# One PSUM chain for MLP and attention, masks on GpSimd, and column-tiled PV for the last token blocks, in a gated mix of sliding attention and token MLP

## The chip, the cores and the metric

The kernel runs on one core of a Trainium2 chip (trn2). The metric is the device time of one execution in microseconds (us), lower is better. The profile's span is some 1.7 us (at most 2.4) shorter than the device time of the same execution; stages below are read from spans. An execution is marked slow when it is over 1.5% above the fastest of its kernel.

## The reference

```python
# x: 1 x 2048 x 512, bf16; 32 heads of 16; window 256; F = 1376
g = sigmoid((x * gate_w).sum(-1, keepdims=True))
q, k, v = split_heads(x @ wqkv)
scores = where(0 <= i - j < 256, q @ k.T * 16 ** -0.5, -1e9)
a = softmax(scores) @ v  -> merge heads -> @ wo
h = layernorm(x)                          # no scale, no bias
u = gelu(einsum("bsd,sf->bdf", h, w1) + b1)   # mixes along the tokens
y = transpose(einsum("bdf,fs->bds", u, w2) + b2)
return g * a + (1 - g) * y
```

## The kernel before

Every operation is recorded as a task with its engine or engines, its buffers and a priority. A list scheduler (`arrange`, with guessed durations) fixes one order before anything is built; each engine then works through its part of that order strictly in sequence. Tokens are in 16 blocks of 128. For each block there are two half tiles of 16 heads, and each half tile has up to three key blocks. One key block is one *score group*: eight row-tiled score matmuls, two exponentials on ScalarE, a mask on two of three, and 16 PV matmuls. There are 90 score groups, in the same order in every kernel of this study. That gives a ruler: the start of score group 24, of 54 and of 89 (the last) marks how far an execution has come, whatever else moved.

```python
# masks: VectorE or GpSimd, as the scheduler finds
got = [add(f"m{qb}.{hf}.{kb}", {"DVE": 1.2, "POOL": 2.1}, emit_m, ex, ORDER["m"], uses=[e])]
# ... PV: e is the stationary operand, 16 matmuls of 128x17, V with a column of ones
# normalise by the sum (17th column)
rc: nc.vector.reciprocal(out=buf(rd)[:], in_=...)
nm: nc.vector.tensor_tensor(out=buf(ob)[...], in0=buf(o)[...], in1=buf(rd)[...], op=ALU.mult)
to: nc.sync.dma_start_transpose(xo[:, qb, :]..., buf(ob))
# ... the gate: g = gg, (1 - g) / 2 = c1, c2 = (1 - g) * b2
ga: nc.scalar.activation(th[:], buf(gb)[:, 0:NT], ACT.Tanh, scale=0.5)
# ... for each token block: two PSUM chains and two passes over 128x512
b, t = chain(f"y{qb}", mms, dw2 + ugr, ORDER["y"] + qb, "y")            # 11 matmuls
yb: affine(buf(bp), buf(b), c1[:, qb:qb + 1], c2[:, qb:qb + 1])         # bp = c1 * y + c2
mms = [(xo[:, qb, c * P:(c + 1) * P], wo[:, c, :], P) for c in range(4)]
b, t = chain(f"a{qb}", mms, [done["ont", qb], dwo, yb], ORDER["a"], "a")  # 4 matmuls
f:  nc.vector.scalar_tensor_tensor(out=buf(ot)[:], in0=buf(b)[:], scalar=gg[:, qb:qb + 1],
                                   in1=buf(bp)[:], op0=ALU.mult, op1=ALU.add)
# ... loads: x0 | K and Q weights, 1 MB | x1 | V weights, 512 KB | x2 | x3
```

(Names before a colon are the tasks' names.)

The softmax here doesn't subtract the row's maximum and nothing guards it: scores larger than these inputs give would overflow.

## Time and profile before

The median is 234.06 us in the rounds of the change (233.92 to 235.37). VectorE is busy 166.4 us, of which 40.4 are masks and 22.5 the two passes at the end of each token block.

And the rows of VectorE that the change touches:

```profile
L602 DVE TENSOR_TENSOR et<-et,mask 128x2048 bf16<-128x2048 bf16 x33 | 40.4, 1231 | 4.0 <-ACT et L591 3.9
...
L538 DVE TENSOR_SCALAR h<-xo,mv,rstd 128x512 bf16<-128x512 bf16 x16 | 13.7, 901 | 0.0
...
L758 DVE SCALAR_TENSOR_TENSOR ot<-pb,gg,bp 128x512 bf16<-128x512 f32 x16 | 12.0, 751 | 6.9 <-PE pb L468 6.9
L317 DVE TENSOR_SCALAR bp<-pb,c,c 128x512 f32<-128x512 f32 x13 | 10.5, 810 | 18.0 <-PE pb L468 18.0
...
L724 DVE SCALAR_TENSOR_TENSOR ug<-t,uf 128x512 bf16<-128x512 f32 (+1 forms) x11 | 9.4, 850 | 5.9 <-ACT t L719 5.9
```

The reader is to see 33 masks of 1.23 us, and means of 0.90 and 0.85 us in the h and ug rows, which are mixtures of undisturbed operations and of ones stretched past 2 us.

### The profile page before, as it was taken

The numbers are of one execution on the slowest core, as the hardware profiler recorded it, in microseconds if no ns is written. First come the engines' busy times: TensorE is split into PE (matmuls) and PEld (weight loads), VectorE is DVE, ScalarE is ACT, GpSimd is POOL, SyncE is SP. The second block draws the span as 40 slices with busy tenths as digits, with TensorE's granted clock in tenths as the row PEclk, the third lists the DMA queues.
The fourth block names the chain that finished last, engine by engine and source line by source line (L and its number), as shares of the span: only waits on it lengthen the run. The fifth ranks groups of instructions, "written<-read, shape, count | busy, mean of one in ns | idle before, by whom it ended". The sixth has DMA issues, their size and how long they took to land.

```text
span 232.9 us, 6602 instructions
## 1 busy us (share of the span) xinstructions
PE 218.2 (94%) x2856; PEld 107.4 (46%) x2856; DVE 166.4 (71%) x255; ACT 192.7 (83%) x220; POOL 66.9 (29%) x50
## 2 busy tenths in 40 slices
PE   7696999979999999999999958999999999999993
PEld 3232444535465444554445523555555555555551
DVE  3779799999877889578899875555565556666522
ACT  2167496778999998996898997999999999999911
POOL 8326534462200003025005100333333333333300
PEclk9799799999999999999999985999999999999999
DMA  6999999002011082010551071010101010301011
GB/s 223 284 209 287 352 345 253 17 0 49 0 25 25 0 312 74 3 25 3 160 226 23 3 246 28 23 48 25 48 24 48 25 45 25 44 28 48 25 46 45
DMA packets 27757, 21.66 MB, mean 93 GB/s; under 512 B 15728, under 2 KB 25456, under 8 KB 27728
## 3 DMA queue, kind: packets, MB, share of 16 engines
q1 hardware_dynamic: 27568, 21.24, 32.4%
q8 instruction: 22, 0.36, 0.6%
q0 software_dynamic: 160, 0.01, 0.5%
q14 instruction: 7, 0.06, 0.1%
HBM read 15.47 MB, written 2.10 MB: 75 GB/s over the span
## 4 chain that ended last, share of the span: by engine, by line
PE 81%; DVE 9%; ACT 4%; DMA 3%; issue 1%; SPq 0%; DVEq 0%; ACTq 0%
PE pb L468 54%; PE pb L627 15%; PE ps L572 12%; DVE h L538 3%; ACT et L591 3%; DMA wqkv<-in_A_wqkv_dram 3%; DVE stats L522 1%; DVE ug L724 1%; DVE QZ L507 1%; DVE b1c L414 1%; PE pb L672 1%; ACT uf L314 1%; ACT t L719 1%; DVE ot L758 0%; DVE KT L433 0%
## 5 line engine op out<-in xcount | busy, mean ns | idle before, releaser
L591 ACT ACTIVATE et<-ps 128x1024 bf16<-128x1024 f32 x180 | 172.1, 1029 | 9.4 <-PE ps L572 8.3
L606 POOL TENSOR_SCALAR_AFFINE_SELECT et<-et 128x2048 bf16<-128x2048 bf16 x27 | 55.1, 2041 | 135.0 <-ACT et L591 130.0
L468 PEld LDWEIGHTS <-wb 128*128 128x128 bf16 (+2 forms) x352 | 30.7, 99 | 39.4 <-issue 11.6
L627 PEld LDWEIGHTS <-et 128*128 128x128 bf16 x1440 | 42.0, 96 | 14.6 <-issue 7.9
L627 PE MATMUL pb<-VA,et 128*128 128x17 bf16 x1440 | 44.6, 171 | 2.4 <-DVE mv L526 2.2
L468 PE MATMUL pb<-ug,wb 128*128 128x512 bf16 (+1 forms) x176 | 44.2, 389 | 0.0
L468 PE MATMUL pb<-h,wb 128*128 128x512 bf16 (+1 forms) x176 | 43.6, 380 | 0.0
L602 DVE TENSOR_TENSOR et<-et,mask 128x2048 bf16<-128x2048 bf16 x33 | 40.4, 1231 | 4.0 <-ACT et L591 3.9
L572 PE MATMUL ps<-QZ,KT 32*128 32x256 bf16 x720 | 36.2, 276 | 3.7 <-ACT et L591 2.3
L468 PE MATMUL pb<-XT,wqkv 128*128 128x512 bf16 x128 | 33.9, 407 | 2.0 <-DMA wqkv<-in_A_wqkv_dram 2.0
L572 PEld LDWEIGHTS <-KT 32*128 32x128 bf16 x720 | 10.8, 92 | 33.4 <-ACT et L591 17.7
L317 DVE TENSOR_SCALAR bp<-pb,c,c 128x512 f32<-128x512 f32 x13 | 10.5, 810 | 18.0 <-PE pb L468 18.0
L507 DVE TENSOR_TENSOR QZ<-pb,par 128x1024 bf16<-128x1024 f32 x16 | 19.0, 1215 | 3.1 <-PE pb L468 2.9
L468 PEld LDWEIGHTS <-wqkv 128*128 128x128 bf16 x128 | 11.9, 102 | 17.2 <-issue 5.0
L643 DVE RECIPROCAL rd<-pb 128x16 f32<-128x16 f32 x32 | 8.1, 254 | 14.5 <-PE pb L627 14.0
L468 PE MATMUL pb<-wqkv,XT 128*128 128x512 bf16 x64 | 16.0, 380 | 1.4 <-DVE VA L433 1.4
L758 DVE SCALAR_TENSOR_TENSOR ot<-pb,gg,bp 128x512 bf16<-128x512 f32 x16 | 12.0, 751 | 6.9 <-PE pb L468 6.9
L468 PE MATMUL pb<-wo,xo 128*128 128x512 bf16 x64 | 16.4, 377 | 0.0
L432 ACT ACTIVATE KT<-pb 128x512 bf16<-128x512 f32 x10 | 6.0, 601 | 12.3 <-PE pb L468 12.3
L650 DVE TENSOR_TENSOR on<-pb,rd 128x256 bf16<-128x256 f32 x32 | 13.5, 423 | 1.0
L538 DVE TENSOR_SCALAR h<-xo,mv,rstd 128x512 bf16<-128x512 bf16 x16 | 13.7, 901 | 0.0
L724 DVE SCALAR_TENSOR_TENSOR ug<-t,uf 128x512 bf16<-128x512 f32 (+1 forms) x11 | 9.4, 850 | 5.9 <-ACT t L719 5.9
(48 smaller groups left out, 99.6 us busy)
## 6 DMA issues: line engine op xcount, KB each, us to landing
wb<-in_B_w_dram SPq DMA_DIRECT2D x8, 512.0 KB, 8.3
wb<-in_B_w_dram SPq DMA_DIRECT2D x2, 2048.0 KB, 8.0
xo<-in_A_x_dram SPq DMA_DIRECT2D x4, 512.0 KB, 9.6
out_dram<-ot SPq DMA_DIRECT2D x16, 128.0 KB, 1.8
wb<-in_B_w_dram SPq DMA_DIRECT2D x4, 352.0 KB, 8.0
wqkv<-in_A_wqkv_dram SPq DMA_DIRECT2D x1, 1024.0 KB, 6.1
wb<-in_B_w_dram SPq DMA_DIRECT2D x1, 1024.0 KB, 5.4
wqkv<-in_A_wqkv_dram SPq DMA_DIRECT2D x1, 512.0 KB, 9.9
```

The source lines that it names most:

```text
L317: return nc.vector.tensor_scalar(out=out_, in0=in_, scalar1=scale, scalar2=bias, op0=ALU.mult, op1=ALU.add)
L468: nc.tensor.matmul(buf(b)[:rows, :], lhsT=lhsT, rhs=rhs, start=(j == 0), stop=(j == n - 1))
L507: lambda k=k, b=b: nc.vector.tensor_tensor(out=QZ[:, i % NQ, k, :, :], in0=buf(b)[:, None, :].to_broadcast([P, 2, SB]), in1=par[:][:, :, N ...
L538: return nc.vector.tensor_scalar(out=h[:, t_, :], in0=xo[:, t_, :], scalar1=mv[:, t_, 0:1], scalar2=rstd[:, t_:t_ + 1], op0=ALU.subtract, ...
L572: made.append(nc.tensor.matmul(buf(b2[r // 2])[:, (r % 2) * 512 + kk * 256:(r % 2) * 512 + kk * 256 + 256], lhsT=KT[32 * r:32 * r + 32, (k ...
L591: lambda j=j, b2=b2, e=e: nc.scalar.activation(out=buf(e)[:, j * 1024:(j + 1) * 1024], in_=buf(b2[j])[:], func=ACT.Exp, scale=SCALE),
L602: return nc.vector.tensor_tensor(out=view, in0=view, in1=mask[:, int(far), None, :].to_broadcast([P, 16, P]), op=ALU.mult)
L606: return nc.gpsimd.affine_select(out=buf(e), in_=buf(e), pattern=[[0, 16], [-1 if far else 1, P]], compare_op=ALU.is_gt if far else ALU.is ...
L627: made.append(nc.tensor.matmul(buf(o)[:, hl * DV:(hl + 1) * DV], lhsT=buf(e)[:, col:col + 128], rhs=VA[:, kb, head, :], start=(first and h ...
L650: lambda rd=rd, o=o, ob=ob, hf=hf: nc.vector.tensor_tensor(out=buf(ob)[:, hf * 256:(hf + 1) * 256].rearrange("p (h d) -> p h d", d=DH), in ...
L724: lambda u=u, t1=t1, fsz=fsz, fc=fc: nc.vector.scalar_tensor_tensor(out=ug[:fsz, fc, :], in0=buf(t1)[:fsz, :], scalar=1.0, in1=buf(u)[:fsz ...
L758: lambda bp=bp, b=b, ot=ot, qb=qb: nc.vector.scalar_tensor_tensor(out=buf(ot)[:], in0=buf(b)[:], scalar=gg[:, qb:qb + 1], in1=buf(bp)[:], ...
```

## The change

Its intent: one pass over PSUM per token block instead of two; a VectorE that has time; fewer TensorE cycles where the tail is. With z the gate logit, g·a + (1-g)·y = (1-g)·(y + e^z·a). So the attention rows are scaled by 2·e^z when they are normalised, accumulate in the same PSUM bank behind the y matmuls, and one affine pass gives the output.

```diff
-                got = [add(..., {"DVE": 1.2, "POOL": 2.1}, emit_m, ex, ORDER["m"], uses=[e])]
+                got = [add(..., {"DVE": 1.2, "POOL": 2.1} if qb >= ORDER["mq"] else {"POOL": 2.1}, ..., two=True)]   # mq = 16
# ... normalise
-            lambda ...: nc.vector.tensor_tensor(out=..., in0=buf(o)..., in1=buf(rd)..., op=ALU.mult)
+            lambda ...: nc.vector.scalar_tensor_tensor(out=..., in0=buf(o)..., scalar=ez[:, qb:qb + 1],
+                in1=buf(rd)..., op0=ALU.mult, op1=ALU.mult)
# ... token blocks from est = 13 on: V stationary, four heads in four column groups
+    nc.tensor.matmul(buf(o)[32 * r:32 * r + 32, at:at + 128], lhsT=VA[:, kb, head * DV:head * DV + 32],
+        rhs=buf(e)[:, col:col + 128], ..., tile_position=(0, 32 * r), skip_group_check=True)
+    # then on VectorE: transpose 32x32 blocks in PSUM, reciprocal, times e^z, times V rows, transpose into xo
# ... the end
-        b, t = chain(f"y{qb}", mms, ...);  yb: bp = c1 * y + c2
-        b, t = chain(f"a{qb}", ...);       f:  ot = gg * a + bp       # VectorE
+        mms += [(xo[:, qb, c * P:(c + 1) * P], wo[:, c, :], P) for c in range(4)]
+        b, t = chain(f"y{qb}", mms, ..., tail=4, tail_deps=rel[qb] + [dwo], ...)
+        f: affine(buf(ot), buf(b), c1, c2)                            # ScalarE or VectorE
# ... loads
-    dwk = load_w("wqk", 0, 2 * D, 0.01)
+    # four loads of 256 KB: K first half, Q first half, (x1), K second half, Q second half
# ... also: XT's blocks serve as probability buffers 5 to 8 once read; the gate in four parts by exp;
#     squares may go to ScalarE; new PSUM bank lists; a model of the shared port and of tile-mode
#     switches in the scheduler; all priorities found anew
```

## The prediction

> **What bounds the kernel now.** I read the page's busy row first, then busy time cut into stages, then the chain of waits, then the timeline of single engines.
>
> ```profile
> PE 218.2 (94%) x2856; PEld 107.4 (46%) x2856; DVE 166.4 (71%) x255; ACT 192.7 (83%) x220; POOL 66.9 (29%) x50
> PE 81%; DVE 9%; ACT 4%; DMA 3%; issue 1%; SPq 0%; DVEq 0%; ACTq 0%
> ```
>
> The second line is the chain that ended last: mostly TensorE. But matmuls overlap, so 94% is not 94% of the work that could be done. The stages say more (columns: busy us of PE, PEld, DVE, ACT, POOL, granted clock, DMA share, GB/s):
>
> ```profile
> 9.20:52.90 43.70, 39.77 (x388) 17.19 (x390) 38.69 (x64) 29.89 (x37) 19.73 (x14) 0.94 0.81 208
> 52.90:136.30 83.40, 82.41 (x1149) 41.80 (x1148) 69.27 (x101) 76.98 (x92) 14.11 (x8) 1.00 0.23 67
> 136.30:150.80 14.50, 11.85 (x171) 5.72 (x175) 9.00 (x13) 13.08 (x15) 2.00 (x1) 0.76 0.32 108
> 150.80:220.20 69.40, 69.40 (x1048) 35.59 (x1048) 41.63 (x60) 68.88 (x73) 24.05 (x12) 1.00 0.15 36
> 220.20:232.90 12.70, 8.83 (x84) 4.43 (x81) 2.94 (x5) 2.33 (x3) 0.00 (x0) 1.00 0.14 42
> ```
>
> The reader should see five stages: projections, where TensorE and VectorE are both full and ScalarE waits; the first MLP layer (TensorE full, ScalarE nearly); a changeover where TensorE idles and its clock falls to 0.76; the second MLP layer, where ScalarE never stops; and a tail of 12.7 us with ScalarE idle. The fourth stage in one line, then one period of it on TensorE:
>
> ```profile
> 149.22 70.94 ACT L591 ACTIVATE et<-ps 128x1024 bf16<-128x1024 f32 x74
> 206.09 0.40 PE L572 MATMUL ps<-QZ,KT 32*128 32x256 bf16 x8
> 206.42 1.90 PE L468 MATMUL pb<-ug,wb 128*128 128x512 bf16 x8
> 208.25 0.40 PE L572 MATMUL ps<-QZ,KT 32*128 32x256 bf16 x8
> 208.58 0.82 PE L468 MATMUL pb<-ug,wb 128*128 128x512 bf16 x3
> 209.24 0.95 PE L627 MATMUL pb<-VA,et 128*128 128x17 bf16 x32
> 210.13 0.40 PE L572 MATMUL ps<-QZ,KT 32*128 32x256 bf16 x8
> ```
>
> 74 exponentials in 70.94 us: 0.95 to 0.96 us each, back to back. From the starts: eight score matmuls 0.33 us, 32 PV matmuls 0.89 us (0.028 each); full 512-column matmuls take 0.216 elsewhere where they are dense. One half tile (3 score groups, 48 PV, 11 of y, 4 of the output projection) is then 0.99 + 1.33 + 2.38 + 0.86 = 5.56 us of TensorE, against six exponentials at 0.95 = 5.7 us. TensorE and ScalarE are almost equally full. A gain must come from idle time of both, not from one engine's sum.
>
> Where is that idle time? Adding the waits between ScalarE's instructions from 9.2 us (first K copy) to 220.2 us (last exponential) gives 21 us: about 14 before 60 us, 7 later. TensorE's own work, 608 wide matmuls x 0.216 + 1440 x 0.028 + 720 x 0.041 + start-up matmuls and gate (about 6), is 207 us; the other 26 us of the span are waits, slow clock and the two ends.
>
> **What the Trainium skill says.** (1) "SBUF — State Buffer", section "Who interferes with whom": VectorE and GpSimd share a port pair as an exclusive lock; a VectorE operation in a two-port mode, or with two SBUF inputs against a GpSimd operation that reads SBUF, blocks or is blocked for the whole instruction. This trace agrees:
>
> ```profile
> 49.11 2.12 DVE L538 TENSOR_SCALAR h<-xo,mv,rstd 128x512 bf16<-128x512 bf16 x1
> 127.30 2.49 DVE L724 SCALAR_TENSOR_TENSOR ug<-t,uf 128x512 bf16<-128x512 f32 x1
> 127.16 2.09 POOL L606 TENSOR_SCALAR_AFFINE_SELECT et<-et 128x2048 bf16<-128x2048 bf16 x1 [0.88 <-POOL et L606]
> ```
>
> Undisturbed, these two VectorE operations take 0.40 and 0.69 us; each was stretched past 2 us by a POOL mask that started just before (POOL's at 49.08 and 127.16). (2) "TensorEngine Tiling (Array Packing)", sections "Key Properties" and "Restrictions": independent tiles run in parallel, a change of tiling mode drains TensorE, and column tiling disables fast weight load. The row-tiled score groups agree on parallelism (eight in 0.33 us; 256 columns are half of the 0.216 us matmul, so eight in sequence would be 0.86). No column tiling is in this trace. (3) "ScalarE: Activation LUTs", section "What ACT_TABLE_LOAD costs": back-to-back activations overlap by about 93 ns. Here a 1.03 us exponential advances ScalarE by 0.95, a 0.60 copy by 0.50.
>
> **The change part by part.** The instruction orders of both builds were compared engine by engine.
>
> *One PSUM chain.* Attention rows are normalised with exp(gate logit) x 2 and accumulated after the 11 y matmuls in the same bank; one scale-and-bias replaces two passes. Removed: 16 final operations on VectorE (12.0 us), the 16 y evictions (13 on VectorE, 10.5 us; 3 on ScalarE). Added: 16 evictions, 14 on VectorE at 0.81 = 11.3 us. Matmul count unchanged. In the second-layer stage VectorE is only 60% busy, so little there is on the path. In the tail it counts: before, 33 wide matmuls, 48 PV and four evictions follow the last exponential.
>
> *Masks.* 33 VectorE masks (40.4 us) go to GpSimd, which then does 60 x 2.04 = 122 us instead of 55. Two per half tile are 4.1 of 5.7 us, so GpSimd keeps up. The price is the lock: 28 GELU operations with two SBUF inputs still on VectorE. GpSimd holding the port 70% of the time, at about 1 us remaining, is 0.7 us each, about 20 us of waiting, plus the 16 normalisations.
>
> *VectorE's sum.* -40.4 (masks) -12.0 -10.5 +11.3 -3.6 (five squares to ScalarE) +4.5 (six bias evictions from ScalarE) +2.7 (gates) and, for six column-tiled half tiles, -4.0 +12 (two transposes, reciprocal, two products, estimated 2 us from the PSUM rows of 0.42 to 0.75): -40 us. 166 becomes 126, some 150 with the blocking.
>
> *ScalarE's sum.* Before, up to the last exponential: 180 x 0.95 + 17 copies x 0.50 + 11 tanh x 0.52 + 6 bias x 0.58 = 188.7. After: 18 copies, 5 squares, 4 tiny gate exponentials: 189. No gain; only its idle time can shrink.
>
> *TensorE's sum.* 288 of 1440 PV matmuls become column-tiled. Four groups side by side, 128 columns in a quarter of 0.216: 16 take at least 0.22 us; with mode change I take 0.32 instead of 0.44, so 18 groups save 2.2 us: 205 us.
>
> *Order and buffers.* The weight load is split, K's first half ahead (256 KB rather than 1 MB), and XT0's copies go to two engines: the first K matmul waited 1.95 us for weights at 7.59; I take 1 us off. Probability buffers 5 to 9 (XT reused), score banks confined to three pairs. Counting TensorE's work between score groups, six groups a stage (before -> after): 18.1 -> 15.5, 12.8 -> 14.1, 13.3 -> 12.4, 13.7 -> 13.7, 14.6 -> 12.0, 12.4 -> 13.7, 13.3 -> 12.0, 9.6 -> 12.2, then 11.1 -> 11.1 to 12.1, and from group 84 to the end 20.5 -> 17.0. ScalarE needs 11.4 to 13.5 in each. The hump at the projections and the hole at the changeover (measured 14.4 us for 9.6 of work, at half clock) are levelled.
>
> *Tail.* After the last exponential: 48 PV (0.2 wait + 1.0), VectorE's chain about 2.4 beside nine y matmuls (1.9), four projections (1.0), eviction 0.8, store to end 3.0 (229.87 to 232.9 now) and waits: 8.7 against 12.7. Saves 4.0.
>
> *Sum.* ScalarE's view: start 8.0 + work 188.5 + idle + tail 8.7. Idle was 21; levelling takes about 6 to 8 (the hump 2.6, the changeover 3, some of the start), the lock gives back 1 or 2: 15. Total 220. TensorE's view: 205 + start 4 + waits to group 12 of 5 + 4 in the first layer + 2 later + 4.5 at the end = 224.5. The middle is 222 of span; the device time is 1.3 above the span now (234.19 against 232.9), and I lean slightly to the ScalarE view: **222.5 us**, 5% faster.
>
> **The rivals.** (a) *The lock binds.* VectorE was already 38.7 of 43.7 us busy in the projection stage, without many masks of its own; with the port held, bias evictions come late, banks stay taken and score groups wait. For: the 2.12 and 2.49 us rows. Against: the new schedule models the port, VectorE loses 40 us, and nine probability buffers absorb late masks. It would give 227 to 236. (b) *Column tiles do not pay.* Without overlap 16 matmuls take 16 x 0.054 = 0.86 us, 8 us more in the final stages, and the transposes add up to 2 us on the last path. For: no fast weight load. Against: row tiles do overlap here. It would give 228 to 231. (c) *The waits nearly vanish.* ScalarE idle falls to 8 us or less: 213 to 215. For: 52.9 to 136.3 has little idle already. Against: the projections need more TensorE than ScalarE whatever the order. (d) *Fewer VectorE passes are hidden anyway.* In the second-layer stage I believe this; then the gain is only tail and levelling, as in my sum.
>
> **Range and chances.** Rival (c) sets the low end and (a) the high: 214 to 230. Two per cent faster is below 229.5. The tail and levelling are separate gains of 4 and 6 us that both would have to fail: faster 0.88, same 0.10, slower 0.02.
>
> **What would show each step right or wrong.** Tail: last exponential to end about 9 us. Levelling: no changeover stage with clock below 0.9; ScalarE idle about 15 us between first K copy and last exponential; exponentials still near 1.03 us each. Lock: the GELU and h rows' mean above 0.9 us and POOL masks at 2.04 or more. Column tiles: 16 PV in 0.25 to 0.40 us. VectorE busy 140 to 155 us, POOL near 135. If ScalarE idle stays above 20 us with waits on evictions, (a) holds; if PV groups of the last three tiles take over 0.6 us, (b).

## More of the kernel before

The granted TensorE clock in 40 slices (tenths; 9 is nine tenths or more):

```profile
PEclk9799799999999999999999985999999999999999
```

Then stages cut at the score-group marks 24, 54 and 89 (columns: stretch, its length, busy us of PE, PEld, DVE, ACT, POOL, granted clock, DMA share, GB/s):

```profile
0.00:79.63 79.63, 72.49 (x820) 33.82 (x821) 65.67 (x114) 57.21 (x72) 29.93 (x32) 0.96 0.57 151
79.63:150.76 71.13, 67.50 (x908) 33.55 (x909) 56.19 (x77) 64.18 (x75) 12.90 (x6) 0.95 0.29 92
150.76:217.59 66.83, 66.83 (x1031) 34.42 (x1031) 39.66 (x58) 66.35 (x71) 23.18 (x12) 1.00 0.15 36
217.59:232.90 15.31, 11.44 (x102) 5.64 (x101) 4.90 (x7) 4.90 (x6) 0.87 (x1) 1.00 0.15 44
```

I call these the start, the first layer (which ends with the changeover to the second), the second layer, and the end.

## The result, and the profile after

The changed kernel is correct. Its four executions took 223.61, 229.18, 224.80 and 230.22 us, median 226.99; the kernel before 234.06. Ratios in this text are the mean time of one kernel's fast runs over that of the other's in the same rounds, so not quite the ratio of the medians quoted: here 0.9567, interval 0.9494 to 0.964. So the sign and the range were right, but half of the executions were in a slower state at a lower clock (1.0 against 0.981). The profiled execution is the 223.61 us one.

Busy row, chain of waits and clock of the page after:

```profile
PE 212.1 (96%) x2856; PEld 101.9 (46%) x2856; DVE 125.7 (57%) x239; ACT 191.4 (86%) x221; POOL 133.1 (60%) x84
...
PEclk9999999999999999999999999999999999999999
...
PE 86%; DMA 6%; ACT 2%; DVE 2%; SPq 1%; issue 1%; ACTq 0%
```

VectorE lost 40.7 us and the share of VectorE in the chain fell from 9% to 2%. The clock has no dip. The same four stages as before:

```profile
0.00:74.17 74.17, 68.97 (x816) 33.36 (x816) 54.36 (x121) 57.00 (x72) 43.55 (x40) 1.00 0.63 163
74.17:140.94 66.77, 66.07 (x908) 32.65 (x908) 43.47 (x61) 64.05 (x76) 40.80 (x21) 1.00 0.29 96
140.94:211.44 70.50, 70.50 (x1054) 33.01 (x1053) 24.94 (x51) 66.82 (x71) 47.13 (x25) 1.00 0.12 36
211.44:221.90 10.46, 6.58 (x81) 2.92 (x80) 2.92 (x7) 3.49 (x4) 1.64 (x1) 1.00 0.08 27
```

Set against before: start -5.5, first layer -4.4, second layer **+3.7**, end -4.9; together -11.0 us of span. The second layer became longer: matmuls that used to stand in the tail now stand there, where TensorE was already full (busy 66.83 of 66.83 before, 70.50 of 70.50 after). TensorE's timelines account for it, counted from start to start: 197 wide (512-column) matmuls begin in this stage instead of 172 (in the end 24 instead of 45) and take 6.35 us more, the PV matmuls take 2.66 us less, since 15 of their groups are column-tiled, and the score matmuls take the same. That makes the 3.7 us.

The column-tiled PV in the tail, TensorE's timeline (start, length, instruction; modelled ends, so starts are compared):

```profile
213.73 0.59 PE L506 MATMUL pb<-ug,wb 128*128 128x512 bf16 x2
214.26 0.41 PE L783 MATMUL pb<-et,VA 128*32 128x128 bf16 x16
214.49 0.40 PE L783 MATMUL pb<-XT,VA 128*32 128x128 bf16 x16
214.71 0.40 PE L783 MATMUL pb<-et,VA 128*32 128x128 bf16 x16
215.04 2.12 PE L506 MATMUL pb<-ug,wb 128*128 128x512 bf16 x9
```

Sixteen start every 0.225 us, so 48 take 0.78 us with the way back to wide matmuls, where 48 of the old kind took 1.33. What it costs on VectorE follows at once:

```profile
215.16 0.73 DVE L799 STREAM_TRANSPOSE pb<-pb 128x512 f32<-128x512 f32 x1 [2.82 <-PE pb L783]
215.93 0.27 DVE L804 RECIPROCAL pb<-pb 128x16 f32<-128x16 f32 x1
...
216.90 0.45 DVE L831 STREAM_TRANSPOSE xo<-zt 128x256 bf16<-128x256 bf16 x1
```

Two products of 0.18 and 0.42 us are left out. 215.16 to 217.35 is 2.2 us, of which nine y matmuls cover 2.0 (215.04 to 217.00). Finally the rows that the lock could stretch (VectorE), and GpSimd's masks:

```profile
L877 DVE SCALAR_TENSOR_TENSOR ug<-t,uf 128x512 bf16<-128x512 f32 (+1 forms) x11 | 11.7, 1066 | 0.1
...
L577 DVE TENSOR_SCALAR h<-xo,mv,rstd 128x512 bf16<-128x512 bf16 x16 | 5.5, 402 | 0.0
```

```profile
L698 POOL TENSOR_SCALAR_AFFINE_SELECT et<-et 128x2048 bf16<-128x2048 bf16 x40 | 80.9, 2029 | 59.1 <-ACT et L683 47.0 <-PE ps L664 6.0 <-PE pb L720 2.2
L698 POOL TENSOR_SCALAR_AFFINE_SELECT XT<-XT 128x2048 bf16<-128x2048 bf16 x20 | 40.1, 2012 | 17.0 <-ACT XT L683 10.9 <-PE ps L664 3.6 <-PE pb L783 1.7
```

The ug row rose from 0.85 to 1.07 us, the h row fell from 0.90 to 0.40, which is undisturbed: the new order keeps h away from masks and pays at the GELU.

### The profile page after: what moved, and what is told of

Its sections match the earlier page's. It is cut to its first block, busy times and chain, and to the rows that moved or that the text cites.

```text
span 221.9 us, 6636 instructions
## 1 busy us (share of the span) xinstructions
PE 212.1 (96%) x2856; PEld 101.9 (46%) x2856; DVE 125.7 (57%) x239; ACT 191.4 (86%) x221; POOL 133.1 (60%) x84
## 4 chain that ended last, share of the span: by engine, by line
PE 86%; DMA 6%; ACT 2%; DVE 2%; SPq 1%; issue 1%; ACTq 0%
PE pb L506 56%; PE pb L720 14%; PE ps L664 13%; DMA wqkv<-in_A_wqkv_dram 4%; PE pb L783 2%; DMA XT<-in_A_x_dram 2%; ACT et L683 2%; SPq L365 1%; PE pb L594 1%; DVE c L629 1%; DVE KT L470 1%; SPq L360 0%; ACT ot L343 0%; ACT VA L469 0%; DVE c L628 0%
## 5 line engine op out<-in xcount | busy, mean ns | idle before, releaser
L683 ACT ACTIVATE et<-ps 128x1024 bf16<-128x1024 f32 x120 | 116.1, 1028 | 8.0 <-PE ps L664 6.6
L698 POOL TENSOR_SCALAR_AFFINE_SELECT et<-et 128x2048 bf16<-128x2048 bf16 x40 | 80.9, 2029 | 59.1 <-ACT et L683 47.0
L683 ACT ACTIVATE XT<-ps 128x1024 bf16<-128x1024 f32 x60 | 58.3, 1027 | 4.6 <-PE ps L664 4.2
L698 POOL TENSOR_SCALAR_AFFINE_SELECT XT<-XT 128x2048 bf16<-128x2048 bf16 x20 | 40.1, 2012 | 17.0 <-ACT XT L683 10.9
L346 DVE TENSOR_SCALAR ot<-pb,c,c 128x512 bf16<-128x512 f32 x14 | 11.3, 810 | 27.9 <-PE pb L506 27.9
L720 PEld LDWEIGHTS <-et 128*128 128x128 bf16 x800 | 23.3, 96 | 7.0 <-issue 3.3
L720 PE MATMUL pb<-VA,et 128*128 128x17 bf16 x800 | 25.5, 171 | 1.0 <-DVE KT L470 1.0
L345 DVE TENSOR_SCALAR uf<-pb,b1c 128x512 f32<-128x512 f32 (+1 forms) x11 | 8.2, 749 | 11.9 <-PE pb L506 11.8
L744 DVE SCALAR_TENSOR_TENSOR on<-pb,ez,rd 128x256 bf16<-128x256 f32 x26 | 12.6, 484 | 0.9 <-DMA xo<-on 0.2
L561 DVE BATCH_NORM_STATS2 stats<-xo 128x6 f32<-128x512 bf16 x16 | 10.6, 681 | 2.6 <-DMA xo<-in_A_x_dram 2.6
```

What stands on the lines that cost most here:

```text
L345: return nc.vector.tensor_scalar(out=out_, in0=in_, scalar1=bias, scalar2=None, op0=ALU.add)
L346: return nc.vector.tensor_scalar(out=out_, in0=in_, scalar1=scale, scalar2=bias, op0=ALU.mult, op1=ALU.add)
L561: f"bs{t_}", {"DVE": 0.67}, lambda b=b, t_=t_: nc.vector.bn_stats(buf(b)[:], xo[:, t_, :]),
L683: lambda j=j, b2=b2, e=e: nc.scalar.activation(out=buf(e)[:, j * 1024:(j + 1) * 1024], in_=buf(b2[j])[:], func=ACT.Exp, scale=SCALE),
L698: return nc.gpsimd.affine_select(out=buf(e), in_=buf(e), pattern=[[0, 16], [-1 if far else 1, P]], compare_op=ALU.is_gt if far else ALU.is ...
L720: made.append(nc.tensor.matmul(buf(o)[:, hl * DV:(hl + 1) * DV], lhsT=buf(e)[:, col:col + 128], rhs=V4[:, kb, head, :], start=(n_ == 0 and ...
```

## The experiments

Three questions were open. Is the gain the change's work, or the clock dips that it happens to remove? Which part makes which stage's gain? And where does the slower half of the executions come from? My theory at first: levelling (an order without humps) and the tail. The rivals: the clock alone, and the lock or VectorE.

Twelve runs were made, all correct, each in five rounds with 6 to 22 executions; one is the changed kernel unaltered. First the table of what they gave; group marks are from the one profiled execution, whatever its state. That is allowed for the three later stages only, because they turned out the same in both states (rows "after" and "unaltered").

| run | median, us | ratio of fast runs | start | first layer | second layer | end |
|---|---|---|---|---|---|---|
| before | 234.06 | 1 | 79.6 | 71.13 | 66.83 | 15.31 |
| after | 226.99 | 0.957 | 74.2 | 66.77 | 70.50 | 10.46 |
| before_warm | 231.29 | 0.988 | 77.7 | 69.76 | 66.83 | 15.38 |
| after_warm | 228.18 | 0.974 | 79.5 | 66.76 | 70.50 | 10.46 |
| after_nocol | 232.26 | 0.992 | 81.9 | 66.77 | 69.47 | 13.32 |
| after_twice | 232.10 | 0.989 | 81.0 | 66.76 | 72.05 | 11.15 |
| after_again (unaltered) | 229.71 | 0.964 | 79.9 | 66.76 | 70.50 | 10.40 |
| after_oneload | 227.82 | 0.963 | 78.5 | 66.77 | 70.50 | 10.14 |
| after_vearly | 229.72 | 0.972 | 83.1 | 66.77 | 70.50 | 10.48 |
| before_split | 239.75 | 1.008 | 85.3 | 71.97 | 66.83 | 15.07 |
| after_fix | 226.69 | 0.970 | 76.8 | 66.77 | 70.50 | 10.47 |
| after_onelate | 224.58 | 0.961 | 77.0 | 66.77 | 70.50 | 10.15 |
| after_mhalf | 232.19 | 0.983 | 78.2 | 69.43 | 70.50 | 10.40 |
| after_onelast | 232.90 | 0.994 | 84.9 | 66.77 | 70.50 | 10.11 |

### before_warm: the old kernel without its clock dips

The kernel before with 33 dummy matmuls of zeros (weight loads 2889 instead of 2856; where 28 is said of them, that is a miscount) put into six of TensorE's waits; every other instruction keeps its order.

```diff
+    fills = {"k0_0.0": 9, "pv0.0.0": 9, "s9.0.9": 4, "s9.0.7": 6, "pv8.1.8": 1, "s9.0.8": 4}
+        for n_, t in enumerate(plan):
+            if fills.get(t.name):
+                fill(n_, fills[t.name])      # matmuls of zeros into a PSUM bank that is free there
```

> The kernel before with 28 dummy 512-column matmuls at six places where TensorE waits (9 ahead of the first K chain, 9 ahead of the first PV group, 15 around the changeover to the second layer), every other instruction in the same order. Clock theory: a good part of the 10.4 us gained comes from the granted clock (0.971 before, 1.0 after); then this alone is 3 to 6 us faster than the kernel before (228 to 231 us) with a clock of 0.985 or more. Levelling theory: the dips fall where other engines set the time; 0 to 1 us faster (233 to 234.5), even at a higher clock.

231.29 us, ratio 0.988 (0.9836 to 0.9925). Its first two stages (the granted clock is the number after POOL's):

```profile
0.00:77.73 77.73, 72.55 (x826) 35.21 (x839) 65.61 (x114) 57.21 (x72) 29.98 (x32) 1.00 0.59 155
77.73:147.49 69.76, 68.33 (x913) 34.29 (x923) 56.17 (x77) 64.18 (x75) 12.91 (x6) 1.00 0.31 94
```

So the dips, and with them what follows from them, cost the old kernel 2.8 us (1.2% of 234), between the two expectations; in the two profiles' stages it is 1.9 in the start and 1.4 at the changeover. "TensorE: Matmul & The Clock Gate" in the Trainium skill, "Part 1: The HAM clock gate", says that a window of idleness of some 3.4 us halves the clock, and that the windows run freely so that the point of the switch varies from run to run. At the changeover of the kernel before, the clock was 0.50 from 137.63 to 144.46 us. In the 3.41 us ahead of that, TensorE was busy for 1.62 us, so about 1.8 us of idleness were enough in this case, less than the page's window. But the sum of the idleness does not decide either: in the control below (after_again) 1.0 us idle in the 3.37 us from 29.60 was followed by half clock, while in after_mhalf 1.6 us idle in the 3.40 us from 136.20 was not. What does decide stays open here. That the clock varies between executions agrees (0.964 to 0.985 in the runs of the kernel before beside this one). This is a measure for what follows: at full clock, from mark 24 to the end, the old kernel needs 151.97 us and the new one 147.73. That is -4.2: first layer -3.0, second layer +3.7, end -4.9.

### after_warm: dummies in the changed kernel's largest early wait

```diff
+    fills = {"v0.0": 8}
```

> The changed kernel with 8 dummy matmuls in the 1.8 us in which TensorE waits for V's weights, nothing else. If the runs of 229 to 230 us at clock 0.981 come from a clock dip after this early wait, all runs are at 223.5 to 225 us with clock 1.0. If the dip starts elsewhere, some runs stay at 229 to 230.

228.18 us, clocks 0.989 to 1.0, start 79.5. The second expectation is the nearer one: no execution is at 225 us or below, and the slowest took 228.97. The dummies did not hold the clock in the profiled execution: TensorE still waited 2.35 us behind them, for V weights that let it go on at 15.93 us, and from 16.47 to 19.89 us the clock was half. But the start is late without that too: one execution had clock 1.0 and still took 226.79 us, against 223.61 and 224.80 for the good executions at the same clock. A slow start is thus a late start first; the clock comes second.

### after_nocol: no column tiles

```diff
-    ... est=13.0 ...
+    ... est=16.0 ...
```

The scheduler places everything anew from there.

> The changed kernel with plain PV for the last three tiles too (rescheduled; the POOL order is the same). My theory: column tiling saves 6 x 0.55 us of TensorE, of which half is on the path, and the tail loses VectorE's short chain for a DMA transpose of over 2 us: 2.5 to 4.5 us slower than the changed kernel (226 to 228 in its fast state), tail over 9.5 us. Rival, that it is worth nothing: within 1 us.

Second layer and end of this run:

```profile
148.71:218.18 69.47, 68.49 (x1029) 35.00 (x1041) 17.86 (x36) 67.20 (x72) 45.93 (x24) 1.00 0.14 38
218.18:231.50 13.32, 9.65 (x93) 4.86 (x93) 1.56 (x4) 3.98 (x5) 2.73 (x2) 0.96 0.14 40
```

Without tiles the end is 2.9 us longer and the second layer 1.0 shorter: the tiles are worth 1.9 us net, under my 2.5 to 4.5 and over the rival's 1. How much of it is TensorE's time and how much the DMA transpose that the tiles avoid is not told apart. The total of 232.26 says more (5 us) only because this run's start is 2 us later than that of the slow unaltered profile; TensorE's weight loads come in the same order for the first 2359 of 2856, up to 184 us in the changed kernel, so the edit is not in the start.

### after_twice: each output bank evicted twice

```diff
+                affine(bp[:], buf(b), c1[:, qb:qb + 1], c2[:, qb:qb + 1]),     # a dummy fp32 pass
                 affine(buf(ot), buf(b), c1[:, qb:qb + 1], c2[:, qb:qb + 1]),
```

> The changed kernel, in which each output bank is evicted twice (a dummy pass of 0.8 us ahead of the real one), nothing else moved: the second VectorE pass that the merged PSUM chain took away, put back. My theory: VectorE has room in the second layer, only the last eviction is on the path: 0.8 to 1.5 us slower. Rival, that the removed pass is the gain: 3 us or more slower.

```profile
147.80:219.85 72.05, 69.16 (x1043) 33.16 (x1056) 34.21 (x63) 67.03 (x71) 47.09 (x25) 1.00 0.12 33
219.85:231.00 11.15, 6.42 (x80) 2.91 (x80) 3.44 (x10) 4.83 (x6) 1.62 (x1) 0.94 0.11 36
```

+1.55 us in the second layer and +0.75 at the end, 2.3 together, although VectorE is busy only 34 of 72 us there. My number was 0.8 to 1.5, the rival's 3 or more; neither holds, and mine missed the larger part. A bank is held longer, and TensorE waited 1.4 us for evictions that it had not waited for. So a second pass is not all hidden here. (In the kernel before, the two passes stood on two banks; here both hold one bank, so this is not the old form put back exactly.)

### after_again: the unaltered changed kernel, as control

> The changed kernel unaltered, as the control of this set. In the earlier sets V's weights landed 8.7 us after issue in the run of 223.6 us, but 11.9 to 12.2 us in three variants, whose TensorE then waited to 16 us and ran at half clock. If that is a state of the changed kernel itself, here too the runs split: 223.5 to 225 with clock 1.0, and 228 to 231 with clock 0.975 to 0.993. If it belongs to the variants, all are at 223.5 to 225.

Six executions from 224.79 to 231.96: the split belongs to the changed kernel itself, as the first expectation has it, though one execution (227.20) lies between the two states. Its profile is of the slow state:

```profile
0.00:79.94 79.94, 72.79 (x818) 34.44 (x819) 54.56 (x121) 57.29 (x72) 43.52 (x40) 0.96 0.64 151
79.94:146.70 66.76, 66.06 (x909) 32.67 (x909) 43.49 (x61) 64.04 (x76) 40.79 (x21) 1.00 0.30 96
146.70:217.20 70.50, 70.50 (x1055) 33.03 (x1055) 24.94 (x52) 66.81 (x71) 47.13 (x25) 1.00 0.12 36
217.20:227.60 10.40, 6.58 (x81) 2.92 (x80) 2.91 (x7) 3.49 (x4) 1.63 (x1) 1.00 0.08 27
```

Compare with the four lines of the good execution: from mark 24 on they agree within 0.07 us. The whole difference between the two states, 5.8 us, is in the start. And its first sign is a load. The issues of the weights in the good execution, then in this one (KB each, us from issue to landing):

```profile
wqkv<-in_A_wqkv_dram SPq DMA_DIRECT2D x4, 256.0 KB, 5.2
...
wqkv<-in_A_wqkv_dram SPq DMA_DIRECT2D x1, 512.0 KB, 8.7
```

```profile
wqkv<-in_A_wqkv_dram SPq DMA_DIRECT2D x4, 256.0 KB, 7.7
...
wqkv<-in_A_wqkv_dram SPq DMA_DIRECT2D x1, 512.0 KB, 12.0
```

The V weights land 3.3 us later, and score group 0 begins at 17.07 instead of 13.72, 3.35 later. The other 2.4 us come later in the start, where this execution has a half-clock stretch (0.62 at 32 to 36 us; another, 0.63 at 8 to 12, lies ahead of group 0). This is one profile of each state. And the late V weights are not all of it: in after_mhalf, whose loads are the same, they landed 7.4 us after issue and group 0 began at 12.42, earlier than in the good execution, and yet the start took 78.2 us. In the rest of the experiments I therefore attack the start.

### after_oneload, after_vearly, before_split: three ways to load the weights

The first issues K and Q weights in one load of 1 MB, as the kernel before did; the second keeps the split but issues all five weight loads ahead of x1; the third gives the split to the kernel before and nothing else.

```diff
# after_oneload
+        if t.name == "wk0":
+            t.emit = lambda: nc.sync.dma_start(wqkv[:, :, 0:2 * D], ...)
+        elif t.name in ("wq0", "wk1", "wq1"):
+            t.emit = lambda: None
# after_vearly: wk1, wq1 and wv moved ahead of x1 in the fixed order
# before_split
+        if t.name == "wqk":
+            t.emit = lambda: part((512, 768), (0, 256))
+        elif t.name == "wv":
+            t.emit = lambda: part((768, 1024), (256, 512), (1024, 1536))
```

> The changed kernel with Q's and K's weights in one load of 1 MB as in the kernel before, all else in the same order. Theory that the split loads (rows of 512 B) delay V's weights in some runs: V's weights land at 12 to 12.5 us in every run, first scores at 14 to 14.5, all runs 224 to 226. Theory that the delay comes from elsewhere in the changed kernel: runs still reach 228 to 231.

> The changed kernel with all five weight loads ahead of the second block of x, all else in the same order. Theory that V's weights wait behind other loads: they land by 10 to 11 us, TensorE does not wait at 11 us, first scores at 12.5 to 13, clock 1.0, all runs 222 to 224, so 1 us below the best of the changed kernel and 5 to 7 below its slow runs. Rival, that the projections are bound by VectorE and the XT transposes: no better than 224.

> The kernel before with the changed kernel's split of the weight loads and nothing else. Theory that this split is a risk and no gain: V's weights land later than 12.3 us in most runs, 234 to 238 us. Rival, that it is part of the gain (the first K matmul at 6.5 us rather than 7.6): 232.5 to 233.5.

One load put the V weights at 7.9 us from issue and group 0 at 12.51, but the median was 227.82 and the executions still reached 230.25, as the second expectation has it. A new wait stood in VectorE's queue (timeline of VectorE, wait in brackets), and behind it one of TensorE:

```profile
18.64 1.32 DVE L452 CAST b2c<-b2t 128x16 f32<-128x16 bf16 x1 [3.02 <-DMA b2t<-in_B_b_dram]
```

```profile
21.42 0.40 PE L664 MATMUL ps<-QZ,KT 32*128 32x256 bf16 x8 [2.79 <-DVE KT L470]
```

A cast of a bias vector that nothing needs before the second layer blocks a K copy that the next score group needs. With the weights early it was worse (229.72, the rival's side), for the same reason with another load:

```profile
14.74 0.69 DVE L561 BATCH_NORM_STATS2 stats<-xo 128x6 f32<-128x512 bf16 x1 [6.46 <-DMA xo<-in_A_x_dram]
```

```profile
16.61 1.89 PE L506 MATMUL pb<-wqkv,XT 128*128 128x512 bf16 x4 [5.25 <-DVE QZ L546]
```

The statistics of token block 4 wait 6.5 us for the x block that was moved back, and the Q copies of block 0 stand behind them. The split alone did not help the old kernel: its two fast executions are 0.8% slower (1.0023 to 1.013), and four of six were slow, with a median of 239.75 us. In the profile, a slow one, the first K chain does start earlier, at 6.95 us instead of 7.59, but then TensorE waits 4.7 us for the V weights. So in the old order the split is no gain: what it wins at the first K chain it loses behind the V weights. "DMA: Bandwidth & Descriptors" of the Trainium skill, "Measured", gives 6.15 us for a load of 1 MB and asks for loads of that size. Its figure is for loads issued from GpSimd and counts the time that the DMA engines are busy; here SyncE issues, and the time is from issue to landing. With this difference the case comes close: 5.8 to 6.1 us for the K and Q weights in one load. Of four quarters, each took a median of 4.8 to 7.7 us. The V weights behind four quarters took 6.9 to 12.2 us over the runs, those behind one load 7.9 to 9.9: behind the split some landed late and some did not, and what makes them late is not shown. (The sets of rounds ran on different chips of the machine, which is not ruled out.)

### after_fix and after_onelate: the same loads with VectorE's early queue put in another order

Both move eight VectorE tasks that wait for x1 or for the biases behind block 0's Q, K and gate work; the first on top of the early weights, the second on top of the one load.

```diff
+    for name in ("bs4", "ba4", "bs5", "bs6", "biases", "ba5", "ba6", "bs7"):
+        move(name, "ba7")        # within the fixed order, ahead of that task
```

> The changed kernel with two edits to the fixed order of the start only: all five weight loads are issued ahead of the second x block, and on VectorE the eight small tasks that wait for that block or for the bias vectors (statistics of tokens 4 to 7, the bias casts) are moved behind the first block's QZ, KT and gate work. Theory (what is left of the two states is work standing in an in-order queue behind a DMA landing, and the half clock that such a pause brings): no TensorE wait above 2 us before the sixth score group, group 12 begins at 45 to 48 us, group 12 to the end still 175 to 176.5, median 222 to 226 with all runs within 1% of it and clocks of 0.99 or more. Rival (the slow starts come from the DMA engines or the chip and not from the order): group 12 at 50 to 53, median 227 to 230, clocks of 0.975 to 0.99 in most runs.

> The other way to the same end: the K and Q weights in one 1 MB load in the place of four of a quarter each, x block order kept, and the same eight VectorE tasks moved back. Its forerunner with the load alone stood 227.8 us with one VectorE wait of 3.0 us for a bias vector. Theory: that wait and the half clock after it go, group 12 begins at 46 to 49 us instead of 50.9, median 223 to 226. Rival (the wait was one of several of equal length): group 12 at 50 to 52, median 227 to 229.

after_fix: group 12 at 48.45 (just outside 45 to 48), 226.69 us, clocks 0.982 to 1.0; better than its forerunner by 3 us (medians of different rounds), but it fits neither theory: a wait of 1.59 us for a transposed x block and half clock at 24 to 28 us (0.50) remained. after_onelate: 224.58 us, and all seven executions lie between 224.38 and 226.07, none slow; group 12 at 49.41 (expected 46 to 49). Its start is 77.0 us in the profiled execution (226.07 us, the slowest of the seven), 2.9 less than that of the slow profile of the unaltered kernel and 2.8 more than that of the good one:

```profile
0.00:76.98 76.98, 69.36 (x806) 33.62 (x818) 54.13 (x121) 57.06 (x72) 43.49 (x40) 0.98 0.62 157
```

It is the version to keep: 4% under the kernel before in the same rounds (0.9608, 0.9565 to 0.965), and, in its seven executions, without the slow half. Against the changed kernel it is not faster than the good executions (223.61, 224.80, 224.79), only steadier; the two did not run in the same rounds, so the difference of the medians (224.58 against 226.99 and 229.71) has no interval.

### after_mhalf: 28 masks back on VectorE

The masks of the far diagonal go back to VectorE, 32 stay on GpSimd; the order of every queue is kept.

```diff
+    for t in plan:
+        if t.name[0] == "m" and t.name.split(".")[0][1:] != t.name.split(".")[-1]:
+            t.engine = "DVE"
```

> The changed kernel with the 28 masks on the far diagonal back on VectorE (32 stay on GpSimd), every queue's order otherwise kept. Theory (with GpSimd at 133 us of 222 the masks' place is not what the time hangs on, and the mask's own delay lies behind other score groups; taking them off VectorE was needed only for its 34 us of queue): group 12 to the end 175 to 177.5, VectorE busy near 160 us, median 227 to 231, that is as the unaltered control. Rival 1 (VectorE's queue was what bound the old kernel): group 12 to the end 178 to 181. Rival 2 (the shared port costs more than the masks' move saves): group 12 to the end under 174.5.

```profile
78.17:147.60 69.43, 65.37 (x899) 32.58 (x909) 53.66 (x72) 64.04 (x76) 20.53 (x10) 1.00 0.28 93
147.60:218.10 70.50, 69.08 (x1043) 33.01 (x1055) 38.29 (x64) 66.68 (x71) 24.05 (x12) 1.00 0.13 36
```

My theory fell and rival 1 held: from group 12 to the end 178.6 us. But the place is narrow. The second layer and the end are the same to 0.06 us, so there it does not matter at all who masks. The first layer takes 69.43 instead of 66.77: nearly the 69.76 of the old kernel at full clock. Of the 3.0 us that the change gains there, 2.7 are gone with half the masks. VectorE's timeline there, the GpSimd mask beside it, and what ScalarE met:

```profile
131.11 1.21 DVE L694 TENSOR_TENSOR XT<-XT,mask 128x2048 bf16<-128x2048 bf16 x1
...
132.90 2.43 DVE L546 TENSOR_TENSOR QZ<-pb,par 128x1024 bf16<-128x1024 f32 x2
135.25 2.47 DVE L865 SCALAR_TENSOR_TENSOR t<-t,uf 96x512 f32<-96x512 f32 x1
```

```profile
135.18 2.00 POOL L698 TENSOR_SCALAR_AFFINE_SELECT et<-et 128x2048 bf16<-128x2048 bf16 x1 [4.54 <-ACT et L683]
```

```profile
137.76 0.63 ACT L872 ACTIVATE t<-t 96x512 f32<-96x512 f32 x1 [2.65 <-DVE t L865]
```

One mask stands ahead of the last GELU's chain at the changeover. The GELU product that took 0.68 us in the changed kernel takes 2.47: a GpSimd mask began 0.07 us before it, and in these traces a GELU operation that meets a mask already begun is the stretched one. ScalarE waits 2.65 us in its own order for it (0.30 in the changed kernel). So the queue and the lock act together, on the one chain that opens the second layer; of the 2.35 us that ScalarE waits longer, the stretch is 1.8. How much each weighs in the 2.7 us of the whole layer is not told apart: the order was made for masks on GpSimd, and an order made for both was not run.

### after_onelast: a step too far

On top of after_onelate, all statistics of token blocks 4 to 10, the biases and two gate tasks go behind the K copies and the normalisation of the first two token blocks.

```diff
+    for name in (
+        "bs4 ba4 bs5 bs6 ba5 ba6 bs7 ba7 bs8 ba8 bs9 ba9 bs10 ba10 biases gates0 gates1".split()
+    ):
+        move(name, "gates2")
+    move("pow1", "m3.0.3")
+    for name in ("h4", "h5", "h6", "h7"):
+        move(name, "qc0_2")
```

> One step on from the version with one K and Q load: VectorE was busy 96% and more of the stretch from 20 to 37 us there, and TensorE and ScalarE stood 1.2 to 2.2 us at a time behind K copies that came after token statistics in its queue. Here all statistics of tokens 4 to 10, the bias casts and the gate arithmetic of blocks 0 and 1 (about 12 us of work, wanted by nothing before score group 12) go behind the K copies and the normalisation of the first two token blocks; the rsqrt task on GpSimd goes back behind the masks of block 2. Theory (the start is bound by VectorE's in-order queue once the loads are in): the waits of TensorE and ScalarE between 20 and 32 us fall by 2 us or more, group 12 begins at 46.5 to 48 us instead of 49.4, group 24 to the end stays 147.4 to 147.8, median 221.5 to 223.5. Rival (TensorE's own work and the x loads bind there, the copies only came last): group 12 at 49 to 50.5, median 224 to 226, and the statistics come to stand before the second block's Q copies instead.

232.90 us: a clear miss, and the rival's last clause names it. Group 6 did come at 30.39 us instead of 33.29, so the early waits did go. Then eight microseconds of statistics, bias casts and gate arithmetic stood in one lump from 31.1 to 39.1 us, ahead of the normalisation that frees a PV bank. VectorE's and TensorE's timelines:

```profile
39.90 0.48 DVE L744 SCALAR_TENSOR_TENSOR on<-pb,ez,rd 128x256 bf16<-128x256 f32 x1
```

```profile
40.44 2.74 PE L506 MATMUL pb<-XT,wqkv 128*128 128x512 bf16 x6 [5.32 <-DVE on L744]
```

Group 12 came at 54.45, 5 us later than without the step. The small tasks that blocked early now blocked later; that spreading them would help is likely from this, but no run shows it.

## Why the prediction was right or wrong

The prediction was right in the sign and in its range; the median came out 4.5 us above 222.5, the good executions 1.1 and 2.3 us above. That these came so near is in part luck: the span fell by 11.0 us, as good as the 11 that follow from the 222 us of span that the text expected, but the second layer and the end gave 1.2 of it instead of 4.0, and a start 5.5 us shorter made up for it. By its steps:

- **Tail: right in size, wrong as a gain.** Last exponential to end: 8.0 us (12.7 before), said 8.7. But the text counted 4.0 us as saved. 3.67 us of them turn up in the second layer, whose y matmuls were pulled ahead of the last exponential; the prediction's own table of TensorE work showed it (20.5 to 17.0 at the end, 11.1 to as much as 12.1 in the stages before), and I took that stage as filled by ScalarE with room to spare, though I had worked out 5.56 against 5.7 us, which leaves 0.3 us per six groups. Second layer and end together gained 1.2 us. This is the term that failed: 25 wide matmuls more in the second layer cost 6.35 us there, and column tiles gave back only 2.66.
- **Levelling: right in kind, smaller.** Said 6 to 8 us. At full clock the first layer with the changeover gained 3.0 us for equal TensorE work (63.6 us by the prediction's stage counts, in both), and after_mhalf shows that 2.7 of them need VectorE free of masks, at least in this order of the queues. The changeover at half clock is gone as said (clock 1.00).
- **Start.** Said to take part of the levelling and 1.2 us of a shorter beginning. It is -5.5 us in a good execution (first K copy at 7.5 instead of 9.2) and +0.3 in a slow one. That the start would have two states was in none of the steps or rivals; it accounts for the distance of the median. The split load that I credited is no gain in the old kernel (before_split).
- **The clock** was seen in the profile (0.76 at the changeover, 0.94 in the projections) and was not made a term; before_warm puts it at 2.8 us.
- **ScalarE's idle**: said 15, is 18.2 in the good execution (21.1 before), counted from the waits that the timeline shows. Its busy sum is unchanged, as said (192.7, 191.4), with four squares where the text said five.
- **VectorE**: the sum of 126 is 125.7. But 20 us of blocking were put on top, and the expected 140 to 155 did not come. The ug row is stretched by 0.38 us on average over 11, the squares (7 at 1.00 us instead of 0.69) by 0.31: 6 us; the h row not at all. So rival (a), that the lock binds, is not what the good execution shows; the slow ones fall into its range of 227 to 236, but by their start.
- **Column tiles**: 0.225 us for 16 instead of 0.32, so rival (b) is out; 1.9 us net.
- **Rival (d)**, fewer VectorE passes are hidden anyway, which I believed for the second layer: false as far as after_twice tells it, where a second pass costs 2.3 us, 1.55 of them in that very layer.
- **Span and device time**: the text added 1.3 us, from the median of 234.19 and the span of an execution that took 234.64. In one and the same execution it is 1.7.

The parts do not add up: 1.9 for the tiles, 2.3 for the pass, 2.7 for half the masks make 6.9 where the whole is 4.2 at full clock. Each was taken out of an order made for all of them; that the reordering itself cost the difference is argued, not shown.

## What to carry to other kernels

A stage in which two engines are nearly equally full has no room for work taken from the tail: count moved work as moved, and only what an idle engine takes as gained. Cut both traces at a ruler that the change does not alter (here the score groups), before explaining a total: it showed that two states 5.8 us apart differ in the start only, and that an unaltered stage behind mark 24 repeats to a tenth of a microsecond. In an in-order queue, a small task that waits for a late load costs what all tasks behind it wait, so put it behind the ones that are urgent, but not in one lump.

## What the Trainium skill lacked or had wrong

- "TensorE: Matmul & The Clock Gate": its rule is about idle gaps over some 3.4 us; short idles between groups of matmuls are named in a later section, without a figure. Here 1.8 us without work in 3.41 us were followed by half clock for 6.83 us (before, 137.63 to 144.46), and 1.0 us once (after_again), but 1.6 us elsewhere were not (after_mhalf). Filling six waits with dummies brought 2.8 us of 234.
- "TensorEngine Tiling (Array Packing)": gives no measured figure for column tiles and nothing on the way back to rows ("TensorE: Matmul & The Clock Gate" has one for three tiles, without the way back). Here 16 matmuls of 128 columns in four column groups start every 0.225 us (0.44 for the untiled form), while the lost fast weight load that it names showed no cost that could be seen; two 32x32 block transposes, of 0.73 us on 128x512 fp32 in PSUM and 0.45 us on 128x256 bf16, and three small VectorE operations (2.2 us in all) go with them.
- "DMA: Bandwidth & Descriptors": its figure for a 1 MB load is for the GpSimd path; from SyncE it took 5.8 to 6.1 us here. It gives no figure for what loads do to the one behind them: 512 KB behind four of 256 KB landed 6.9 to 12.2 us after issue, and 7.9 to 9.9 behind one of 1 MB.
